# Phi in the place of its transposed softmax, its exponentials in the split keys' place, and the softmax step ahead of the last mixing step

## The chip, the core and the metric

One core of a Trainium2 chip runs the whole kernel as one program. The metric is the device time of one execution in microseconds (us), median of several runs. The engines are TensorE (PE; its weight loads are PEld), VectorE (DVE), ScalarE (ACT), GpSimd (POOL) and SyncE (SP), whose queue issues the DMAs. Each engine works through its own row of instructions in order; between engines they wait for each other.

## What is computed

```python
# q, k, v: (8 batches, 8 heads, 576, 64); phi: (8, 8, 576, 32)
a = exp(phi - max(phi, axis=2)); a = a / (sum(a, axis=2) + 1e-09)      # softmax over the 576 rows
k_m = einsum('bhsm,bhsd->bhmd', a, k); v_m = einsum('bhsm,bhsd->bhmd', a, v)
scores = matmul(q, k_m^T) / sqrt(64); attn = softmax(scores) ; x = matmul(attn, v_m)
X = fft over the 576 rows, then over the 512 columns; u = x + real(X)
un = (u - mean) / sqrt(var + 1e-06)                                    # per row
out = u + relu(un @ w_ch1) @ w_ch2                                     # 512 -> 2048 -> 512
```

Phi's softmax makes 32 memory slots a head; each row of q attends to those 32 slots. The result, all heads side by side, is 8 x 576 rows of 512, mixed by two Fourier transforms, normalized and sent through a two-layer FFN.

## The kernel before

**Tiles and chunks.** The 4608 rows are 36 tiles of 128 rows. A batch gives 4.5 tiles: two mixing steps (`t0`, `t1`) each give two tiles, one for either sign of the frequency, and step `t2` gives half a tile, whose other half comes from the next batch. An even batch mixes `t0`, `t1`, `t2`; an odd batch `t2`, `t0`, `t1`, so that its `t2` completes the tile the even batch began. Two tiles are a chunk, and there are 18 chunks. Chunk 6 is tiles 12 and 13, and tile 13 is completed by batch 3's `t2`; chunk 15 is completed by batch 7's `t2` in the same manner.

**The FFN.** For each chunk `norm_chunk` (L864) normalizes both tiles: ACT makes mean and variance (L853, L854), DVE and POOL the factor (L855 to L859), DVE the normalized tile `un` (L860). Then ACT casts to 16 bits (`ud`, L879), POOL makes the low half (L880), and a DMA transposes both (L882 by L301) into `unring`. The first layer's matmuls `ph` (L318, eight groups of 24 a chunk) read `unring`; ACT and DVE make the high and low half of the relu in `hring` (L939, L940); the second layer's matmuls are `po` (L949). Up to seven hidden blocks of the first layer run ahead of the second.

**Attention and mixing of a batch** are the generator `background()` (L1175), of which the main loop takes a step now and then between the FFN's blocks (`advance`). A batch's steps are in order: the softmax of phi (`pooling_weights`), four pairs of heads (`pair_memory`, then the scores `psc`), `values`, `spectrum` (matmuls `pa`), and three mixing steps (matmuls `pp` for the Fourier part, `px` for the attention part; ACT L818 and DVE L821, L835 add them into the tile).

**The softmax step** `pooling_weights` (L385): four loads bring phi to `phs`; PE transposes (`pf_b_0`, `pf_b_1` with four transposes of 128 columns each, `pl_b` with the rest of both); DVE takes maxima (L398, L403 to L405); ACT makes four exponentials into `pht`, a view of `phs` (L409, L410); DVE sums and inverts (L411 to L415). Then, for g = 0 and 1, ACT and DVE make the high and low half in `elt` (L418, L419), and a DMA transposes `elt` into `et`. There is one `elt`, so its second filling waits for the first transpose. Batches 0 and 1 take another way, in 32 bits.

**Pairs.** `pair_memory` (L516) squares keys, values and queries on ACT to find their size (L526, L529). The squares themselves are dumped into `stg[:, 2]`, where the split keys are to lie later; a matmul with ones (`pm` <- small) adds the sums across partitions, ACT and POOL or DVE split keys and values in halves (L541 to L547), and 20 matmuls `pm` <- `et`, `stg` make the memory.

**Places.** `phs` is reused inside a batch: `stacks[2]` and `stacks[3]`, the transposed scores of pairs 2 and 3, are views of it, and the mixing matmuls `px` read them until the batch's last mixing step. So the loads of the next batch's phi wait for that step. `et` is last read by the `pm` matmuls of a batch's fourth pair.

A framework sorts the instructions into each engine's row beforehand, from the order in which the program issues them and its own estimate of when each can start. So the rows follow the program's order only roughly, and code that is issued elsewhere changes rows of other stages too.

Of the kernel before, what the change touches and what calls it, by code (L numbers as in the profile page):

```python
# [10 lines left out]
F32 = mybir.dt.float32  # L11
# [10 lines left out]
B, H, S, D, M = 8, 8, 576, 64, 32  # L22
NG = H // 2
# [114 lines left out]
def kernel(  # L138
# [70 lines left out]
    def of_kind(t, w):  # L209
        return t[:, :, 1:3] if w else t[:, :, 0::3]  # L210

    qs = [stg[:, 2, 2 * nk + i * NQ : 2 * nk + (i + 1) * NQ] for i in range(2)]
    et32 = et.rearrange("p g l t c -> p (g l t c)").bitcast(F32).rearrange("p (g t c) -> p g t c", g=2, t=NST)


# [107 lines left out]


    def load_phi(b):
        for g in range(NG):
            nc.sync.dma_start(out=phs[:, :, g], in_=raw[b, g, :, KV:KVP].rearrange("p (t c) -> p t c", t=NST))

    def load_pair(b, g):
        r = rawt  # L330
# [53 lines left out]

    def pooling_weights(b):  # L385

        if b:
            load_phi(b)
        pl = psg.tile([P, 512], F32, tag="g", name=f"pl_{b}")
        mx = tiny("mx", 4, 2)  # L390
        pf = []
        for g in range(2):
            pf.append(psg.tile([P, 512], F32, tag="g", name=f"pf_{b}_{g}"))
            for t in range(NST):
                dst = pf[g][:, t * P : (t + 1) * P] if t < 4 else pl[:, g * P : (g + 1) * P]
                marks["pe"] = nc.tensor.transpose(dst, phs[:, t, 2 * g : 2 * g + 2].rearrange("p g c -> p (g c)"), identf)
            if b >= NX:
                nc.vector.tensor_reduce(out=mx[:, g : g + 1], in_=pf[g], axis=AX.X, op=ALU.max)  # L398
        rest = pl[:, : 2 * P].rearrange("p (g s) -> p g s", g=2)[:, :, : S - 4 * P]
# [775 lines left out]
    def background():  # L1175
# [3 lines left out]
        for b in range(B):  # L1179
            n = f"{b}"  # L1180
            ivs = tiny("ivs", NG)
            mem, ahl = {}, {}
            if b != 1:
                pooling_weights(b)
            yield (nt if half_made is None else half_made), 0
            if b == 0:

                for g in range(NG + 1):
# [7 lines left out]
            for step in range(NG + 2) if b > 0 else ():  # L1196
# [7 lines left out]
                if step < NG:  # L1204
                    mem[step] = pair_memory(b, step, r, vmf, ivs)
                    yield (nt if half_made is None else half_made), 0
            vbd, vh, isg, igx, isq = values(b, vmf, ivs, ahl)
            yield (nt if half_made is None else half_made), 0
            at = spectrum(b, aeo)
            if b == 0:  # L1210
# [2 lines left out]
            for g in sorted(ahl):  # L1213
                pair_transpose(b, g, ahl.pop(g), attnT)
            full = slice(0, P)
            for t in (0, 1, 2) if b % 2 == 0 else (2, 0, 1):
                yield (nt if half_made is None else half_made), 2 if t < 2 else 1 - b % 2
                if t == 2:
                    if b % 2 == 0:
                        u2 = uring[:, len(allocs) % NU]  # L1220
                        us[nt] = u2
                        allocs.append(nt)
                        half_made = nt
                        nt += 1
                    rows = slice(64 * (b % 2), 64 * (b % 2) + 64)
                    tm = mix_m(b, "t2", slice(256, 320), rows, at, vh, isg, isq)
                    px = mix_x(b, "t2", 4 * P + 64, 64, rows, attnT, vbd)
                    add_mix(u2, rows, px, igx, tm, 0)
                    half_made = nt - 1 if b % 2 == 0 else None
                    continue  # L1230
                tm = mix_m(b, f"t{t}", slice(t * P, (t + 1) * P), full, at, vh, isg, isg)
                for sign in range(2):
                    c0 = (2 * t + sign) * P
                    px = mix_x(b, f"t{t}{sign}", c0, P, full, attnT, vbd)
                    u = uring[:, len(allocs) % NU]
                    allocs.append(nt)
                    add_mix(u, full, px, igx, tm, sign)
                    us[nt] = u
                    nt += 1
            yield (nt if half_made is None else half_made), 0  # L1240
        while True:
            yield n_tiles, 0
# [209 lines left out]
```

## Time and profile before

| | |
|---|---|
| time, median of 3 runs | 923.89 us (922.73 to 924.33) |
| profiled execution, its own time | 923.03 us |
| its span, first to last instruction | 921.2 us |
| PE busy | 909.5 us, 99% |
| DVE, ACT, POOL busy | 618.0, 492.2, 268.3 us |
| PE's waits for `et` | 2.4 us in three places |
| mean granted clock of TensorE | 0.998 of full speed |

The span is what the trace covers; 1.8 us of the execution lie outside it. PE is nearly always busy. Its busy time counts matmuls from start to modelled end, so that a PE at half its clock also counts as busy: what a stretch was worth is seen in the granted clock beside it (1.00 is the 2.4 GHz level, 0.50 the 1.2 GHz one).

### The profile page before, as it was taken

The numbers are of one execution on the slowest core, as the hardware profiler recorded it, in microseconds if no ns is written. First come the engines' busy times: TensorE is split into PE (matmuls) and PEld (weight loads), VectorE is DVE, ScalarE is ACT, GpSimd is POOL, SyncE is SP. The second block draws the span as 40 slices with busy tenths as digits, with TensorE's granted clock in tenths as the row PEclk, the third lists the DMA queues.
The fourth block names the chain that finished last, engine by engine and source line by source line (L and its number), as shares of the span: only waits on it lengthen the run. The fifth ranks groups of instructions, "written<-read, shape, count | busy, mean of one in ns | idle before, by whom it ended". The sixth has DMA issues, their size and how long they took to land.

```text
span 921.2 us, 19338 instructions
## 1 busy us (share of the span) xinstructions
PE 909.5 (99%) x7796; PEld 671.5 (73%) x7796; DVE 618.0 (67%) x1471; ACT 492.2 (53%) x955; POOL 268.3 (29%) x302
## 2 busy tenths in 40 slices
PE   9999899999999999999999999999999999999998
PEld 8977577677766766776767666777776777688887
DVE  5979967677577775787554767567765776564554
ACT  5658867655464654664444545466546644443331
POOL 1305524124154231463143423144213141400000
PEclk9999999999999999999999999999999999999999
DMA  9938732433336342545123524163416335210000
GB/s 326 413 146 284 208 91 52 97 84 105 60 75 166 76 124 55 144 84 148 40 69 64 159 72 123 41 141 110 96 38 158 76 106 150 47 46 2 24 14 34
DMA packets 132761, 100.16 MB, mean 109 GB/s; under 512 B 115008, under 2 KB 115264, under 8 KB 130624
## 3 DMA queue, kind: packets, MB, share of 16 engines
q1 hardware_dynamic: 132672, 98.93, 39.4%
q8 instruction: 61, 1.00, 0.5%
q14 instruction: 28, 0.23, 0.1%
HBM read 62.35 MB, written 13.63 MB: 82 GB/s over the span
## 4 chain that ended last, share of the span: by engine, by line
PE 79%; DVE 8%; ACT 4%; DMA 3%; issue 3%; POOL 2%; SPq 1%; POOLq 0%; ACTq 0%; DVEq 0%
PE ph L318 32%; PE po L949 26%; PE po L1011 6%; PE pm L318 2%; PE pp_t L318 2%; PE psc L318 2%; PE po L910 1%; PE pa L748 1%; DMA et<-elt 1%; PE ph L893 1%; POOL ud L880 1%; DMA w1t<-in_raw 1%; PE pm L497 1%; PE px_t L318 1%; DVE w2s L1100 1%
## 5 line engine op out<-in xcount | busy, mean ns | idle before, releaser
L318 PE MATMUL ph<-unring,w1t 128*128 128x256 f16 x3264 | 389.7, 273 | 0.0
L318 PEld LDWEIGHTS <-w1t 128*128 128x128 f16 x3264 | 314.9, 98 | 58.0 <-issue 3.1
L949 PE MATMUL po<-w2s,hring 128*128 128x512 f16 x1344 | 309.2, 379 | 0.5 <-DVE uring L1056 0.5
L949 PEld LDWEIGHTS <-hring 128*128 128x128 f16 x1344 | 129.9, 98 | 134.1 <-issue 0.6
L940 DVE SCALAR_TENSOR_TENSOR hring<-ph,hring 128x512 f16<-128x512 f32 x112 | 76.0, 681 | 25.2 <-ACT hring L939 23.7
L939 ACT ACTIVATE hring<-ph 128x512 f16<-128x512 f32 x112 | 65.7, 588 | 47.3 <-PE ph L318 46.9
L859 POOL TENSOR_TENSOR scratch<-scratch,small 128x1 f32<-128x1 f32 x36 | 23.9, 667 | 174.7 <-DVE scratch L858 162.5
L634 POOL TENSOR_TENSOR aring<-aring,scratch 128x384 f32<-128x384 f32 x28 | 26.2, 934 | 164.7 <-DVE scratch L632 141.0
L880 POOL TENSOR_TENSOR ud<-un,ud 128x1024 f16<-128x1024 f32 x17 | 37.2, 2186 | 35.8 <-ACT ud L879 35.8
L318 PEld LDWEIGHTS <-stg 128*128 128x128 f16 x912 | 35.2, 97 | 6.5 <-issue 3.3
L628 ACT ACTIVATE aring<-aring,scratch 128x384 f32<-128x384 f32 x24 | 14.6, 610 | 47.2 <-DVE aring L627 47.1
L658 ACT CAST aeo<-eo 128x384 f16<-128x384 f32 x30 | 15.3, 511 | 42.1 <-DVE eo L655 42.1
L835 DVE SCALAR_TENSOR_TENSOR uring<-px_t,scratch,share 128x256 f32<-128x256 f32 (+1 forms) x80 | 34.2, 477 | 1.5 <-PE px_t L318 1.5
L821 DVE SCALAR_TENSOR_TENSOR share<-pp_t,scratch,small 128x257 f32<-128x257 f32 (+1 forms) x48 | 21.1, 480 | 20.3 <-ACT small L818 20.1
L618 DVE TENSOR_REDUCE scratch<-psc 128x12 f32<-128x384 f32 x32 | 17.6, 552 | 24.6 <-PE pm L318 19.7
L544 POOL TENSOR_TENSOR stg<-rawt,stg 128x640 f16<-128x640 f32 x12 | 18.6, 1548 | 52.9 <-ACT rawt L543 52.8
L910 PE MATMUL po<-w2s,hring 128*128 128x512 f32 x64 | 31.2, 609 | 1.9 <-ACT hring L896 1.9
L646 ACT CAST at<-aring 128x640 f16<-128x640 f32 x28 | 20.2, 722 | 23.4 <-POOL aring L634 23.4
L1033 POOL TENSOR_TENSOR uring<-uring,share 128x256 f32<-128x256 f32 x3 | 2.2, 726 | 102.3 <-ACT share L1030 102.3
L660 DVE SCALAR_TENSOR_TENSOR aeo<-aeo,small,eo 128x128 f16<-128x128 f16 x30 | 24.4, 812 | 10.1 <-ACT aeo L658 10.1
L651 DVE TENSOR_TENSOR eo<-aring 128x128 f32<-128x128 f32 x29 | 25.6, 882 | 7.7 <-POOL aring L649 7.7
L659 POOL TENSOR_TENSOR aeo<-eo,aeo 128x256 f16<-128x256 f32 x30 | 22.4, 748 | 28.0 <-ACT aeo L658 24.8
(320 smaller groups left out, 1560.3 us busy)
## 6 DMA issues: line engine op xcount, KB each, us to landing
out<-uring SPq DMA_DIRECT2D x35, 256.0 KB, 2.3
rawt<-in_raw SPq DMA_DIRECT2D x13, 640.0 KB, 5.0
stg<-in_raw SPq DMA_DIRECT2D x13, 640.0 KB, 4.9
stg<-in_w SPq DMA_DIRECT2D x7, 1024.0 KB, 6.1
rawt<-in_raw SPq DMA_DIRECT2D x15, 384.0 KB, 3.1
stg<-in_raw SPq DMA_DIRECT2D x15, 384.0 KB, 3.2
phs<-in_raw SPq DMA_DIRECT2D x28, 160.0 KB, 3.2
w2s<-in_w SPq DMA_DIRECT2D x4, 1024.0 KB, 10.8
```

The lines of the kernel that those rows point to most:

```text
L318: m = nc.tensor.matmul(out, lhsT=lhsT, rhs=rhs, start=start, stop=stop)
L634: eng.tensor_tensor(out=a, in0=a, in1=sm.unsqueeze(2).to_broadcast([P, 12, M]), op=ALU.mult)
L651: nc.vector.tensor_tensor(out=eo[:, 1:3, 0], in0=ap[:, 1:3, 0], in1=ap[:, 1:3, 1], op=ALU.add)
L660: marks[f"s{b}_{g}"] = nc.vector.scalar_tensor_tensor(out=lo[:, :4], in0=hi[:, :4], scalar=mk[:, 64:65], in1=eov[:, :4], op0=ALU.mult, op1 ...
L835: nc.vector.scalar_tensor_tensor(out=u[rows, hs], in0=px[rows, hs], scalar=igx[rows], in1=tm[rows, w * NJ + half : w * NJ + half + 256], o ...
L859: nc.gpsimd.tensor_tensor(out=rs, in0=rs, in1=half, op=ALU.pow)
L880: marks[f"ul{c}"] = nc.gpsimd.tensor_tensor(out=ud[:, 1], in0=un, in1=ud[:, 0], op=ALU.subtract)
L910: nc.tensor.matmul(po[t], lhsT=h[:, f, t], rhs=w[:, f], start=(j == 0 and f == 0), stop=(j == NW - 1 and f == UB - 1),)
L939: marks["fa"] = nc.scalar.activation(h[:, 0], phv, AF.Relu)
L940: marks["fd"] = nc.vector.scalar_tensor_tensor(out=h[:, 1], in0=phv, scalar=0.0, in1=h[:, 0], op0=ALU.max, op1=ALU.subtract)
L949: nc.tensor.matmul(po[t], lhsT=hs[j][:, lh, f * 2 + t], rhs=w2s[:, j * UB + f, lw, :], start=(j == 0 and f == 0 and i == 0), stop=(j == NW ...
L1011: m = nc.tensor.matmul(po[n], lhsT=h[:, la, a], rhs=b[lb], start=(j == 0 and i == 0 and n in ("p1", "p6", "p5", "p4")), stop=(j == NW - 1 ...
```

## The change

For batches after the first, phi is loaded into `phi_own`, a 32-bit view of `et`, in place of `phs`, and its exponentials are written into `pht_own`, a 32-bit view of the first part of `stg[:, 2]`, in place of the view of `phs`. The loads of batch b+1 are issued in the step of `values(b)`, when `et` has been read. `pooling_weights(b + 1)` is issued in a step of its own ahead of batch b's last mixing step for b from 2 to 6, and for batch 2 at the end of batch 1. The number of steps of a batch stays the same, and so do number and form of the instructions. All lines behind the first hunk get numbers two or three higher.

```diff
+    pht_own = stg[:, 2].bitcast(F32)[:, : 2 * S].rearrange("p (g s) -> p g s", g=2)
     qs = [stg[:, 2, 2 * nk + i * NQ : 2 * nk + (i + 1) * NQ] for i in range(2)]
+    phi_own = et.rearrange("p g l t c -> p (g l t c)").bitcast(F32).rearrange("p (t g c) -> p t g c", t=NST, g=NG)
...
     def load_phi(b):
+        dst = phi_own if b else phs
         for g in range(NG):
-            nc.sync.dma_start(out=phs[:, :, g], in_=raw[b, g, :, KV:KVP].rearrange("p (t c) -> p t c", t=NST))
+            nc.sync.dma_start(out=dst[:, :, g], in_=raw[b, g, :, KV:KVP].rearrange("p (t c) -> p t c", t=NST))
...
     def pooling_weights(b):
 
-        if b:
-            load_phi(b)
+        phi, pht = (phi_own, pht_own) if b else (phs, None)
...
-                marks["pe"] = nc.tensor.transpose(dst, phs[:, t, 2 * g : 2 * g + 2].rearrange("p g c -> p (g c)"), identf)
+                marks["pe"] = nc.tensor.transpose(dst, phi[:, t, 2 * g : 2 * g + 2].rearrange("p g c -> p (g c)"), identf)
...
-            if b != 1:
+            if b == 0:
                 pooling_weights(b)
-            yield (nt if half_made is None else half_made), 0
+            if b < NX:
+                yield (nt if half_made is None else half_made), 0
...
             vbd, vh, isg, igx, isq = values(b, vmf, ivs, ahl)
+            if 0 < b < B - 1:
+                load_phi(b + 1)
...
-            for t in (0, 1, 2) if b % 2 == 0 else (2, 0, 1):
+            for i, t in enumerate((0, 1, 2) if b % 2 == 0 else (2, 0, 1)):
+                if i == 2 and 1 < b < B - 1:
+                    yield (nt if half_made is None else half_made), 0
+                    pooling_weights(b + 1)
                 yield (nt if half_made is None else half_made), 2 if t < 2 else 1 - b % 2
...
+            if b == 1:
+                yield (nt if half_made is None else half_made), 0
+                pooling_weights(2)
             yield (nt if half_made is None else half_made), 0
```

How the rows move is seen in three places. The first is PE's row from batch 3's mixing (`px_3_t..`) and the softmax transposes of batch 4 (`pf_4`, `pl_4`) to chunk 6's first layer (`ph_6_0`). Before, the transposes stand among chunk 5's second layer (`po_5_0`, `po_5_1`), right ahead of `ph_6_0`:

```order
L949 MATMUL po_5_1_4019<-w2s_102,hring_106 128x512
L396 MATMUL pf_4_1_4247<-identf_88,phs_72 128x128 x4
L396 MATMUL pl_4_4239<-identf_88,phs_72 128x128
L318 LDWEIGHTS small_86
L318 MATMUL pm_4_0_4315<-scratch_112,small_86 128x3
L949 LDWEIGHTS hring_106
L949 MATMUL po_5_1_4019<-w2s_102,hring_106 128x512
L949 LDWEIGHTS hring_106
L949 MATMUL po_5_1_4019<-w2s_102,hring_106 128x512
L318 LDWEIGHTS w1t_101
L318 MATMUL ph_6_0_4203<-unring_105,w1t_101 128x256
```

In the changed kernel they stand inside the mixing, and the mixing runs straight into `ph_6_0`:

```order
L320 MATMUL px_3_t01_4090<-vbdt_78,phs_72 128x64
L398 MATMUL pf_4_0_4141<-identf_88,et_74 128x128 x4
L398 MATMUL pl_4_4140<-identf_88,et_74 128x128 x2
L398 MATMUL pf_4_1_4148<-identf_88,et_74 128x128 x4
L320 LDWEIGHTS at_80
L320 MATMUL pp_3_t1_4232<-vh_79,at_80 128x257
...
L320 LDWEIGHTS phs_72
L320 MATMUL px_3_t11_4259<-vbdt_78,phs_72 128x64
L320 LDWEIGHTS w1t_101
L320 MATMUL ph_6_0_4200<-unring_105,w1t_101 128x256
```

The `po_5` matmuls have moved in front of batch 3's mixing; from `px_3_t2` to `ph_6_0` there is none left.

The second is ACT's row at the same place. `un_84` and `ud_85` are the normalized tile and its halves, `small_86` the mixing's scratch. Before, the cast into `ud` (L879) follows the two passes over the tile directly:

```order
L818 ACTIVATE small_86<-pp_3_t2_3931,scratch_112 64x255
L818 ACTIVATE small_86<-pp_3_t0_4059,scratch_112 128x255
L853 ACTIVATE un_84,scratch_112<-uring_87 128x512
L854 ACTIVATE un_84,scratch_112<-uring_87,scratch_112 128x512
L879 CAST ud_85<-un_84 128x1024
L818 ACTIVATE small_86<-pp_3_t1_4136,scratch_112 128x255
L853 ACTIVATE un_84,scratch_112<-uring_87 128x512 x2
L854 ACTIVATE un_84,scratch_112<-uring_87,scratch_112 128x512 x2
L879 CAST ud_85<-un_84 128x1024
L409 ACTIVATE phs_72,scratch_112<-pf_4_0_4240,scratch_112 128x512
```

In the changed kernel the exponentials and the next mixing step's pass stand in between:

```order
L820 ACTIVATE small_86<-pp_3_t2_3935,scratch_112 64x255
L820 ACTIVATE small_86<-pp_3_t0_4063,scratch_112 128x255
L855 ACTIVATE un_84,scratch_112<-uring_87 128x512
L856 ACTIVATE un_84,scratch_112<-uring_87,scratch_112 128x512
L411 ACTIVATE stg_100,scratch_112<-pf_4_0_4141,scratch_112 128x512
L412 ACTIVATE stg_100,scratch_112<-pl_4_4140,scratch_112 128x64
L411 ACTIVATE stg_100,scratch_112<-pf_4_1_4148,scratch_112 128x512
L412 ACTIVATE stg_100,scratch_112<-pl_4_4140,scratch_112 128x64
L820 ACTIVATE small_86<-pp_3_t1_4232,scratch_112 128x255
L881 CAST ud_85<-un_84 128x1024
L420 ACTIVATE elt_73<-stg_100,scratch_112 128x576
```

The cast (now L881) has moved behind the four exponentials (L411, L412) and `pp_3_t1`'s pass.

The third is ACT's row behind batch 3's exponentials. `stg_100` holds split keys and queries, `rawt_71` the loaded ones. Before, the split of pair 0 (L541, L603) stands ahead of the first `elt`, its squares still further ahead:

```order
L409 ACTIVATE phs_72,scratch_112<-pf_3_1_3013,scratch_112 128x512
L410 ACTIVATE phs_72,scratch_112<-pl_3_3005,scratch_112 128x64
L541 ACTIVATE stg_100<-rawt_71,scratch_112 128x5x2x64
L541 ACTIVATE stg_100<-rawt_71,scratch_112 128x5x128
L603 ACTIVATE stg_100<-rawt_71,scratch_112 128x768
L418 ACTIVATE elt_73<-phs_72,scratch_112 128x576
L939 ACTIVATE hring_106<-ph_4_0_2969 128x512
L543 ACTIVATE rawt_71<-rawt_71,scratch_112 128x5x128
L939 ACTIVATE hring_106<-ph_4_1_3048 128x512
L969 CAST ud_85<-un_84 128x1024
L418 ACTIVATE elt_73<-phs_72,scratch_112 128x576
```

In the changed kernel the squares of pair 0 (L528, L531) come only behind the second `elt`, and the split (L543) behind those:

```order
L420 ACTIVATE elt_73<-stg_100,scratch_112 128x576
L941 ACTIVATE hring_106<-ph_4_0_2977 128x512
L941 ACTIVATE hring_106<-ph_4_1_3048 128x512
L420 ACTIVATE elt_73<-stg_100,scratch_112 128x576
L528 ACTIVATE stg_100,scratch_112<-rawt_71 128x5x2x64
L528 ACTIVATE stg_100,scratch_112<-rawt_71 128x5x128
L531 ACTIVATE stg_100,scratch_112<-rawt_71 128x768
L971 CAST ud_85<-un_84 128x1024
L941 ACTIVATE hring_106<-ph_4_2_3132 128x512
L941 ACTIVATE hring_106<-ph_4_3_3213 128x512
L543 ACTIVATE stg_100<-rawt_71,scratch_112 128x5x2x64
```

What stood beside the softmax's chain has moved behind it.

## Rows read from the trace of the kernel before

**Rows 1.** The page: span, and busy time of PE (share, instructions).

```profile
span 921.2 us, 19338 instructions
...
PE 909.5 (99%) x7796; PEld 671.5 (73%) x7796; DVE 618.0 (67%) x1471; ACT 492.2 (53%) x955; POOL 268.3 (29%) x302
```

**Rows 2.** Waits of PE: releaser: us in total, times, longest.

```profile
PE pm L318 <- DMA et<-elt: 2.4, 3, 1.9
```

**Rows 3.** Timeline of PE, batch 3: start, duration, instruction, [idle before <- releaser].

```profile
280.80 0.69 PE L318 MATMUL pm<-et,stg 128*128 128x64 f16 x20 [1.91 <-DMA et<-elt]
```

**Rows 4.** Windows: from:to, length, busy PE, PEld, DVE, ACT, POOL, PEclk, DMA share, GB/s.

```profile
281.80:282.80 1.00, 1.00 (x8) 0.76 (x6) 0.96 (x3) 1.00 (x4) 0.00 (x0) 0.60 0.91 293
282.80:283.80 1.00, 1.00 (x7) 0.72 (x5) 0.51 (x3) 1.00 (x5) 0.00 (x0) 0.50 1.00 371
283.80:284.80 1.00, 1.00 (x7) 0.69 (x6) 0.58 (x2) 0.61 (x2) 0.00 (x0) 0.50 1.23 344
284.80:286.00 1.20, 1.20 (x10) 0.96 (x9) 1.20 (x2) 0.00 (x0) 0.00 (x0) 0.74 1.14 220
```

**Rows 5.** Timeline of PE: last softmax transpose of batch 3.

```profile
266.20 0.27 PE L396 MATMUL pl<-identf,phs 128*128 128x128 f32 x1
```

**Rows 6.** Tile `et`: who waited for it, us in total, times.

```profile
  ACT elt L418: 18.9, 6
```

**Rows 7.** Timeline of PE, batch 3 mixing to chunk 6.

```profile
352.80 0.29 PE L318 MATMUL px_t<-vbdt,phs 96*64 96x64 f16 x4
353.02 1.49 PE L318 MATMUL pp_t<-vh,at 128*128 128x257 f16 x12
354.34 0.28 PE L318 MATMUL px_t<-vbdt,attnT 96*128 96x64 f16 x4
...
354.58 3.40 PE L949 MATMUL po<-w2s,hring 128*128 128x512 f16 x15
...
366.96 0.60 PE L396 MATMUL pf<-identf,phs 128*128 128x128 f32 x4
...
367.51 0.81 PE L949 MATMUL po<-w2s,hring 128*128 128x512 f16 x3
...
369.16 1.03 PE L318 MATMUL ph<-unring,w1t 128*128 128x256 f16 x8
```

**Rows 8.** Timelines of DVE, ACT and POOL in the same stretch, in this order.

```profile
357.75 0.55 DVE L860 TENSOR_SCALAR un<-uring,scratch 128x512 f32<-128x512 f32 x1 [0.66 <-POOL scratch L859]
358.26 0.88 DVE L835 SCALAR_TENSOR_TENSOR uring<-px_t,scratch,share 128x256 f32<-128x256 f32 x2
...
358.33 1.04 ACT L879 CAST ud<-un 128x1024 f16<-128x1024 f32 x1 [1.64 <-DVE un L860]
359.57 0.47 ACT L818 ACTIVATE small<-pp_t,scratch 128x255 f32<-128x255 f32 x1 [0.19 <-PE pp_t L318]
...
359.46 2.13 POOL L880 TENSOR_TENSOR ud<-un,ud 128x1024 f16<-128x1024 f32 x1 [1.74 <-ACT ud L879]
```

**Rows 9.** Tile `unring`: its transposes from issue to landing.

```profile
DMA to landing us min/median/max: 3.6/4.2/5.6
```

**Rows 10.** Timelines: a maximum (DVE), exponentials of two pairs (ACT, batch 2).

```profile
367.60 0.69 DVE L398 TENSOR_REDUCE scratch<-pf 128x1 f32<-128x512 f32 x1 [1.38 <-PE pf L396]
...
167.15 0.69 ACT L409 ACTIVATE phs<-pf,scratch 128x512 f32<-128x512 f32 x1 [1.97 <-DVE scratch L405]
...
168.12 0.68 ACT L409 ACTIVATE phs<-pf,scratch 128x512 f32<-128x512 f32 x1
```

**Rows 11.** Timelines of POOL and DVE in batch 2; line L404: min/median/max ns.

```profile
164.77 2.12 POOL L1161 TENSOR_TENSOR w2s<-w2s 128x1024 f16<-128x1024 f32 x1 [1.30 <-ACT w2s L1160]
...
164.89 2.02 DVE L404 TENSOR_TENSOR scratch<-scratch 128x2 f32<-128x2 f32 x1
...
L404 DVE TENSOR_TENSOR scratch<-scratch x6: 153/161/2025, 164.9 to 699.8; 128x2 f32<-128x2 f32 x6
```

**Rows 12.** Timeline of PE: second layer ahead of chunk 15.

```profile
786.16 10.74 PE L949 MATMUL po<-w2s,hring 128*128 128x512 f16 x49
```

## The prediction

> **What bounds the kernel now.** I read the busy times first: PE works 909.5 of 921.2 us [rows 1], so a change gains only what PE idles or runs slowly, and loses whatever makes PE idle anew. Second, the waits of PE: the one that this change is aimed at, `pm` waiting for the transposed softmax `et`, is 2.4 us in three places, 1.9 of it in batch 3 [rows 2]. Third, the windows, which show a price that the waits hide: behind that 1.9 us idle [rows 3] the granted clock, full in the 25 us ahead, falls to 0.60, 0.50, 0.50 and 0.74 in four neighbouring windows [rows 4]. That is 0.80 + 1.00 + 1.00 + 0.62 = 3.4 us at the lower level (1.2 instead of 2.4 GHz), in which half is lost: 1.7 us. All that can be won at `et` is therefore 2.4 + 1.7 = **4.1 us**. Last, I read where PE is next to idle: at the first matmul of a chunk's FFN, which needs that chunk's normalized tiles. Nothing waits there in this run, because other PE work lies between; how much does is what the change alters.
>
> **What the change takes away.** Phi of the next batch no longer waits for the last mixing step to leave `phs`. In batch 3 the last softmax transpose ends at 266.20 + 0.27 = 266.5 and the `et` matmuls start at 280.8: the chain takes 14.3 us [rows 3, 5], and PE has 12.4 of work in it. In the changed order the PE work between the same two points, counted in matmuls at the widths and pitches of these rows, is 21 us or more in batches 2, 3, 5, 6 and 7, so the wait goes there: -2.4 - 1.7 = **-4.1 us**. In batch 4 it is only about 11.5, which by itself would leave 3, but that stretch holds the new wait computed below, which covers it. The instructions themselves are the same in number and form; of the four loads a batch, SP has none that stands in front of a transpose PE needs soon: 0.
>
> **What it adds: a wait for the split keys' place.** The squares of pair 0 (`pair_memory`) write into `stg[:, 2]`, which now holds the exponentials until the second `elt` is made, and this waits for the first `et` transpose (ACT already waits 18.9 us there in six steps [rows 6]). So the conversion of pair 0 no longer runs beside the softmax: the ones-matmul of pair 0 in batch 3 moves from right behind the softmax transposes to 16 us of PE work later, and the whole attention of batch 3 ends some 15 us later in PE's row. The four later steps from ones-matmul to `et` matmuls keep 4.4 us of PE work or more, as pairs 1 to 3 have today without a wait: no cost of its own. But what is late next is the mixing of batch 3, and with it chunk 6, whose second tile is finished by `px_3_t2`.
>
> **Chunk 6, the term that decides.** Today 53 `po` matmuls of chunk 5 lie between `px_3_t2` and `ph_6_0`, and PE is occupied from 353.09 to 369.16, 16.1 us [rows 7]. In the new order chunk 5 is used up before `pp_3_t2`, and between the two stand only two mixing products, four sets of `px`, and the ten transposes of the softmax step, which is now in front of the last mixing step. By starts in the rows: 353.02 to 354.34 = 1.32 a product; 354.34 to 354.58 = 0.24 a set; 366.96 to 367.51 = 0.55 for five transposes [rows 7]. 2 x 1.32 + 4 x 0.24 + 2 x 0.55 = **4.7 us** of work.
> Against it stands the chain from `px_3_t2` to the landing of `unring`. Today: DVE normalizes until 358.30, ACT casts until 359.37, POOL makes the low half until 361.59 [rows 8], that is 361.59 - 353.09 = 8.5 us; with the transpose's 4.2 us [rows 9] 12.7. In the new order two things stand inside it. On DVE two maxima over 512 columns (0.69 each), one over the rest, two small operations (0.16 each) and two additions that came later before (0.88) stand ahead of the normalization; with 0.3 for the smaller maximum (an estimate: a quarter of the columns and the start) that is 2 x 0.69 + 0.3 + 0.32 + 0.88 = 2.9, of which 0.4 fills a gap, so 2.5 [rows 8, 10, 11]. On ACT the exponentials of two pairs (one pair 167.15 to 168.12, so 1.94 [rows 10]) and one `L818` (0.47 [rows 8]) stand ahead of the cast; the exponentials wait for the last maximum, and the normalization runs beside the first half of them, so 1.5 remains. Chain: 12.7 + 2.5 + 1.5 = 16.7; PE is out of work after 4.7: **+12.0 us**. Lower end: if nothing of the softmax step delays it, 12.7 - 4.7 = 8.0. Upper end: +1.4 if the transpose lands in 5.6 instead of 4.2 [rows 9], and +1.9 as follows.
> One row shows that a DVE operation over two columns, of 0.16 us normally, took 2.02 us, from 164.89 to 166.91, while POOL ran from 164.77 to 166.89 [rows 11]: it ended when POOL did. The same operation is now in the normalization's way; 2.02 - 0.16 = 1.9. I take 0, since POOL's row at that place has only the step that waits for this normalization. The Trainium skill, SBUF — State Buffer, section SBUF: two separate sides, says that a DVE operation with two SBUF inputs and a GpSimd operation that reads SBUF take a shared port pair in turn, and the loser stands still for the whole instruction; the row agrees, and by this rule the sum would become 1.9 larger if POOL were busy there.
> An idle of 12 us at `ph_6_0` is longer than the 1.9 of batch 3, and I give it the same price in clock: **+1.7 us** (no less; 0 only if the clock stays).
> The first `relu` of chunk 6 then stands on ACT behind the second `elt` and the squares. These need no PE work, so they run on while PE is idle for the 12 us, and that idle is their cover: 0, or 2 us if the cover is a little short (an estimate: three squares, each about an exponential's 0.69 [rows 10]).
>
> **Chunk 15** is finished by `px_7_t2` in the same way. Between it and `ph_15_0` stand two products, four sets and 36 `po` matmuls; 49 of these take 10.74, 0.22 each [rows 12]: 2.64 + 0.96 + 7.9 = 11.5 us. Its chain has none of the softmax in it, so 12.7: **+1.2 us**; bounds 0 and 1.2 + 1.4 (slow landing) + 1.7 (clock). The smallest such distance of another chunk is about 15, against 12.7: no wait.
>
> **Sum.** -4.1 + 12.0 + 1.7 + 1.2 = +10.8 us. The profiled execution took 923.03 (span 921.2), so 933.8; the median 923.89 lies 0.86 above it: **934.7 us**.
>
> **Rivals.**
> A (the sum), 934.7: 0.62.
> B, the other side: the `et` waits go and chunk 6's chain is covered, 923.9 - 4.1 = 919.8. It is one place, `ph_6_0`, and turns on the exposure there staying under about 4 us, that is on a chain below 8.8 us. For it: PE is as good as never idle in this profile. Against it: cast, low half and transposition alone are 1.0 + 2.1 + 4.2 = 7.3 of it, and nothing in the new order could give PE more than 4.7 us of work: 0.07.
> C, only the unavoidable part: 8.0 at chunk 6 with the clock, none at 15: -4.1 + 9.7 = +5.6, 929.5; without the clock 927.8. For it: DVE and ACT have gaps in these rows into which the softmax step may fall: 0.18.
> D, all upper ends: 1.9 + 1.4 at chunk 6 and 1.4 + 1.7 at chunk 15: +10.8 + 6.4 = +17.2, 941.1. For it: one landing in the list took 5.6; against: they must coincide: 0.10.
> E, the change doesn't do what it says: the `et` chain finds its load or its exponentials late again in batch 3, and the 4.1 us stay: 938.9. For it: `elt` is still single, and its second half still waits for a landing; against: 21 us of work against 14.3: 0.03.
>
> **How the numbers follow.** Likeliest A: 934.7. The range from 927 to 941 takes in C with and without the clock, E, and nearly all of D; B and the far end of D are left out. About 0.2% (1.85 us) is what a measurement here can tell from no change. Faster is most of B, 0.06; within 0.2% the rest of B and the lower edge of C, 0.04; slower A, most of C, D and E, 0.90.
>
> **What would show it.** Right: no `pm <- et` wait in batches 2 and 3; a wait of PE at the first `ph` of chunk 6 of 10 to 14 us with the `unring` transpose named last; 16 to 17 us from `px_3_t2` to it, with the maxima and exponentials inside; a half-clock stretch of 3 to 4 us behind it; a small wait at chunk 15. Wrong: FFN matmuls of chunk 5 still running between `px_3_t2` and `ph_6_0`, or an idle below 5 us there, which is B; an idle of 8 with the cast right behind the normalization is C; a new wait at another engine that I have not named would make the sum itself wrong.

## The result and the profile after

The changed kernel takes 936.52 us (median of 4 runs, 936.16 to 936.62), the one before 923.31 beside it (4 runs): ratio 1.0142, interval 1.0125 to 1.016. It is slower by 13.2 us. The forecast was 934.7, range 927 to 941. The profiled execution took 936.61 us with a span of 934.8, 13.6 more than the span before.

The first view to read is again the list of PE's waits, now of the changed kernel (engine, line, what it waited for: us in total, times, longest us):

```profile
PE ph L320 <- DMA unring<-ud: 11.8, 1, 11.8
...
PE ph L320 <- DVE un L862: 1.5, 1, 1.5
PE pa L742 <- DVE aeo L662: 1.3, 1, 1.3
PE pm L320 <- ACT stg L543: 0.8, 1, 0.8
```

The waits for `et` [rows 2] are gone. In their place stands one wait of 11.8 us at the first layer, and behind it small ones: 1.5 at the first layer again (this is chunk 15), 1.3 at `pa` in batch 1 and 0.8 at `pm` in batch 3, the last two new and not forecast. The rows left out are short or stand in the kernel before with nearly the same length. The long one in PE's timeline (start us, duration, instruction, idle before and what ended it), with the rows that answer to [rows 7]:

```profile
364.92 0.29 PE L320 MATMUL px_t<-vbdt,phs 96*64 96x64 f16 x4
...
369.73 0.28 PE L320 MATMUL px_t<-vbdt,phs 96*128 96x64 f16 x4
381.77 8.06 PE L320 MATMUL ph<-unring,w1t 128*128 128x256 f16 x48 [11.76 <-DMA unring<-ud]
```

`px_3_t2` ends at 364.92 + 0.29 = 365.21. PE has work until 370.01, which is 4.8 us, and chunk 6 starts at 381.77: the chain took 16.56 us. Where the kernel before has 53 `po` matmuls in between there is none left.

What the chain is made of, in the timelines of DVE, ACT, POOL and SP in this order (they answer to [rows 8]):

```profile
371.93 0.55 DVE L862 TENSOR_SCALAR un<-uring,scratch 128x512 f32<-128x512 f32 x1 [0.32 <-POOL scratch L861]
...
371.70 0.69 ACT L411 ACTIVATE stg<-pf,scratch 128x512 f32<-128x512 f32 x1 [2.88 <-DVE scratch L407]
...
373.97 1.06 ACT L881 CAST ud<-un 128x1024 f16<-128x1024 f32 x1
...
375.11 2.13 POOL L882 TENSOR_TENSOR ud<-un,ud 128x1024 f16<-128x1024 f32 x1 [3.22 <-ACT ud L881]
...
377.27 1.78 SPq L303 DMA_TRANSPOSE unring<-ud  x1
```

The tile is normalized at 371.93 + 0.55 = 372.48, 7.3 us behind `px_3_t2` (5.2 before). The first exponential starts at 371.70, and the cast, ready at 372.48, waits for the exponentials until 373.97. POOL's low half ends at 377.24, the transpose is issued at 377.27 and PE starts 4.5 us later.

Behind the wait stands the slow stretch, in the windows (from:to, length, busy time of PE, PEld, DVE, ACT and POOL, then the granted clock, DMA share, GB/s):

```profile
372.00:374.00 2.00, 0.00 (x0) 0.00 (x0) 0.67 (x3) 2.00 (x10) 0.00 (x0) 0.90 0.00 0
...
382.00:384.00 2.00, 2.00 (x11) 1.40 (x10) 0.02 (x1) 1.74 (x2) 0.96 (x1) 0.50 0.32 59
384.00:386.00 2.00, 2.00 (x12) 1.34 (x11) 1.78 (x1) 0.18 (x1) 1.92 (x2) 0.50 0.00 0
386.00:388.00 2.00, 2.00 (x14) 1.53 (x13) 0.00 (x0) 2.00 (x5) 1.92 (x2) 0.69 0.49 95
```

From 381.77 the clock is at the lower level for 0.23 + 2.00 + 2.00 + 1.24 = 5.5 us, 2.7 lost. It had fallen while PE stood idle: 0.90 from 372 to 374, 0.50 from there on. In [rows 4] the stretch was 3.4 us, behind a shorter idle, and it began only when PE had worked again for 1 us (from 280.80 to 281.80 the clock is 1.00).

The sum against the profile before: -2.4 and -1.7 at `et`, +11.8 at chunk 6, +2.7 of clock, +1.5 at chunk 15, +1.3 at `pa`, +0.8 at `pm`; the other small waits come to about -0.6. Together 13.4 of the 13.6 us.

### The profile page after: what moved, and what is told of

It is laid out like the page before. It is cut to its first block, busy times and chain, and to the rows that moved or that the text cites. A ratio compares the mean times of both kernels' runs of the same rounds, so it can differ in the third digit from the quotient of the medians.

```text
span 934.8 us, 19333 instructions
## 1 busy us (share of the span) xinstructions
PE 910.9 (97%) x7796; PEld 670.8 (72%) x7796; DVE 619.1 (66%) x1471; ACT 494.5 (53%) x955; POOL 267.6 (29%) x302
## 4 chain that ended last, share of the span: by engine, by line
PE 88%; DVE 4%; ACT 3%; DMA 2%; issue 1%; SPq 1%; POOL 1%; ACTq 0%
PE ph L320 37%; PE po L951 30%; PE po L1013 6%; PE pm L320 2%; PE pp_t L320 2%; PE psc L320 2%; PE po L912 1%; PE pa L750 1%; PE ph L895 1%; DMA w1t<-in_raw 1%; PE px_t L320 1%; PE pm L499 1%; DMA et<-elt 1%; PE pp_t L801 1%; DVE w2s L1102 1%
## 5 line engine op out<-in xcount | busy, mean ns | idle before, releaser
L320 PE MATMUL ph<-unring,w1t 128*128 128x256 f16 x3264 | 390.4, 274 | 13.2 <-DMA unring<-ud 11.8
L823 DVE SCALAR_TENSOR_TENSOR share<-pp_t,scratch,small 128x257 f32<-128x257 f32 (+1 forms) x48 | 21.1, 480 | 24.3 <-ACT small L820 24.2
L837 DVE SCALAR_TENSOR_TENSOR uring<-px_t,scratch,share 128x256 f32<-128x256 f32 (+1 forms) x80 | 34.2, 476 | 1.2 <-PE px_t L320 1.1
L546 POOL TENSOR_TENSOR stg<-stg 128x640 f16<-128x640 f32 x12 | 19.3, 1607 | 50.6 <-ACT stg L545 50.6
L895 PE MATMUL ph<-unring,w1t 128*128 128x256 f32 x128 | 30.6, 383 | 0.0
```

The source lines that it names most:

```text
L320: m = nc.tensor.matmul(out, lhsT=lhsT, rhs=rhs, start=start, stop=stop)
L546: nc.gpsimd.tensor_tensor(out=lo, in0=kinds[w], in1=hi, op=ALU.subtract)
L837: nc.vector.scalar_tensor_tensor(out=u[rows, hs], in0=px[rows, hs], scalar=igx[rows], in1=tm[rows, w * NJ + half : w * NJ + half + 256], o ...
L895: nc.tensor.matmul(ph, lhsT=w[:, k, f * P : (f + 1) * P], rhs=unTs[0][:, k], start=(k == 0), stop=(k == NK - 1))
```

## The experiments

**Theory.** Pair 0's squares and split wait for the place in which the exponentials lie. This moves a batch's attention back in PE's row by some 15 us, and the FFN work that covered the next chunk's normalization is used up before it is needed. **Rival.** The softmax step, now ahead of the last mixing step, stands inside the normalization's chain and lengthens it. Besides, what phi's own place is worth was to be seen alone. The change has three parts, which the runs put together in different ways:

| kernel | phi in | exponentials in | softmax step | us |
|---|---|---|---|---|
| before | `phs` | `phs` | behind the last mixing step | 923.3 to 923.5 |
| run e5 | `phs` | split keys' place | behind | 968.05 |
| run e1 | `et` | split keys' place | behind | 960.92 |
| changed | `et` | split keys' place | ahead | 936.52 |
| run e6 | `et` | `phs` | behind | 919.47 |
| run e2 | `et` | scores' ring | ahead | 919.48 |
| run e3 | `et` | scores' ring | ahead of the first mixing step | 925.28 |

**Both places, the order as before.**

```diff
-                if i == 2 and 1 < b < B - 1:
-                    yield (nt if half_made is None else half_made), 0
-                    pooling_weights(b + 1)
...
-            if b == 1:
+            if 0 < b < B - 1:
                 yield (nt if half_made is None else half_made), 0
-                pooling_weights(2)
+                pooling_weights(b + 1)
```

> The changed kernel, but the softmax step of the next batch stands behind the batch's last mixing step, as before; phi in et and the exponentials in the split keys' place stay. Theory (the new wait for the split keys' place starves PE): slower still than the changed kernel. In PE's row only 4.5, 4.8 and 5.6 us of work stand between the finishing mix and the first layer of chunks 6, 13 and 15, and 11.7 at chunk 11, against a chain of 12.7 without the softmax in it: idles of about 8.2, 7.9, 7.1 and 1.0, each of the first three with 2 to 3 us of lost clock, so 923.3 - 4.1 + 24 + 8 = about 951 us. Rival (the softmax step inside the normalization's chain is what costs): the chain is free of it again, so 920 to 924 us.

Measured: 960.92 us, ratio to the kernel before 1.0405 (1.0389 to 1.0422). PE's waits:

```profile
PE ph L320 <- DVE un L862: 11.4, 1, 11.4
PE ph L320 <- DMA unring<-ud: 11.4, 2, 9.6
PE ph L320 <- ACT un L856: 11.1, 1, 11.1
```

Three waits of 9.6 to 11.4 us at the first layer (chunks 6, 13 and 15), and a fourth of 1.9 (chunk 11), where the changed kernel has one long and one of 1.5. So the softmax step's new order isn't what costs; without it the kernel is 24 us slower still. The theory's direction held, its size didn't: it allowed 7 to 8 us a wait, because it took the chain for 12.7 us when the softmax isn't in it. Chunk 15 shows that this is too little: no softmax step follows batch 7, and yet its chain takes 15.4 us, from the end of `px_7_t2` at 820.58 to

```profile
827.79 0.54 DVE L862 TENSOR_SCALAR un<-uring,scratch 128x512 f32<-128x512 f32 x1
...
835.99 2.31 PE L320 MATMUL ph<-unring,w1t 128*128 128x256 f16 x10 [9.57 <-DMA unring<-ud]
```

The tile is normalized 7.8 us behind `px_7_t2`, where it takes 5.2 at chunk 15 of the changed kernel. Run e4 shows what stands in between.

**The exponentials in a place of their own.**

```diff
-    pht_own = stg[:, 2].bitcast(F32)[:, : 2 * S].rearrange("p (g s) -> p g s", g=2)
+    pht_own = aring.rearrange("p n c m -> p (n c m)")[:, : 2 * S].rearrange("p (g s) -> p g s", g=2)
```

> The changed kernel, but the exponentials lie in the scores' ring aring, which is idle there, instead of in the split keys' place; the order in which the steps are issued stays. Theory: pair 0 no longer waits, chunk 6 gets 13.6 us of PE work in front of it against 16.7 with the softmax in its chain (idle up to 3), and the et matmuls of batches 4 and 6 have 12.7 and 12.6 us against 14.3 (idle up to 1.7 each): 923.3 - 4.1 + 3 + 3.4 = about 925, between 919 and 929. Rival (the softmax step's place costs it): chunk 6 idles 8 us or more as in the changed kernel, 930 to 937 us.

Measured: 919.48 us, ratio 0.9955 (0.994 to 0.9971), better than expected and faster than both kernels. The order in which the steps are issued is that of the changed kernel; only the place differs. Behind the first 140 us PE's waits are these alone:

```profile
PE psc L320 <- DVE scratch L589: 0.8, 2, 0.4
```

Neither the wait at chunk 6 nor one for `et` is left, so the order of issue alone doesn't cost. It doesn't settle by itself what the softmax step costs inside the chain, because here it isn't inside. DVE's row at chunk 6:

```profile
354.20 0.55 DVE L862 TENSOR_SCALAR un<-uring,scratch 128x512 f32<-128x512 f32 x1 [0.67 <-POOL scratch L861]
...
355.50 0.68 DVE L400 TENSOR_REDUCE scratch<-pf 128x1 f32<-128x512 f32 x1
```

The normalization stands ahead of the maxima and ends at 354.75, 5.2 us behind `px_3_t2` (349.54) as in the kernel before; with FFN matmuls between the mixing steps the framework orders the row the other way round. That price is for run e4.

**The same, the softmax step ahead of the first mixing step** (`if i == 0` in place of `if i == 2`).

> As the run with the exponentials in the scores' ring, and the softmax step is issued ahead of the batch's first mixing step instead of its last. Theory: 16.8 us of PE work in front of chunk 6, 15.3 to 17.7 at chunks 4, 11, 13 and 15, 19 us or more ahead of the et matmuls of batches 3 to 7 (15.0 in batch 2): neither wait is left, 923.3 - 4.1 = about 919 us, 918 to 922. Rival (softmax in front of mixing lengthens the chain): 927 us or more.

Measured: 925.28 us, ratio 1.0026 (1.0015 to 1.0038). The expectation missed by 6 us: `et` and chunk 6 are free as expected, but other waits came up.

```profile
PE psc L320 <- DVE scratch L589: 3.5, 3, 1.6
```

There is also one of 1.4 us at `po`. What those at `psc` hang on is seen in batch 3, POOL's and DVE's timelines:

```profile
274.91 2.12 POOL L962 TENSOR_TENSOR un<-w2s 128x1024 f32<-128x1024 f16 x1
...
274.95 2.37 DVE L579 TENSOR_SCALAR vmf<-scratch 64x32 f32<-64x32 f32 x2
277.24 0.74 DVE L589 TENSOR_TENSOR scratch<-scratch 128x64 f16<-128x64 f32 x1
```

Two small DVE operations take 2.37 us together, until 277.32, while a POOL operation runs from 274.91 to 277.03; the scores' `psc` wait for the operation that follows. The two other waits at `psc` have the same rows: the DVE pair takes 2.38 us from 375.86 beside POOL's 375.83 to 377.95, and 2.37 from 605.41 beside 605.38 to 607.50. So it is where POOL's long operations fall, moved by the new order, and not the chain of chunk 6. The wait at `po` wasn't followed.

**Batch 3 alone with the softmax step behind.**

```diff
-                if i == 2 and 1 < b < B - 1:
+                if i == 2 and 1 < b < B - 1 and b != 3:
...
-            if b == 1:
+            if b in (1, 3):
                 yield (nt if half_made is None else half_made), 0
-                pooling_weights(2)
+                pooling_weights(b + 1)
```

> The changed kernel, but in batch 3 alone the softmax step of batch 4 stands behind the last mixing step. PE's work in front of chunk 6 is 4.5 us as in the changed kernel. Theory: only the part of the chain that the softmax step adds goes, 16.6 to about 12.7, so the idle at chunk 6 falls from 11.8 to about 8.2 and the time from 936.5 to about 933 us. Rival: the whole idle goes, about 923 us.

Measured: 935.46 us, ratio 1.0128 (1.011 to 1.0146), one us less than the changed kernel. PE's, DVE's and ACT's timelines:

```profile
364.94 0.29 PE L320 MATMUL px_t<-vbdt,phs 96*64 96x64 f16 x4
...
381.11 8.08 PE L320 MATMUL ph<-unring,w1t 128*128 128x256 f16 x48 [11.08 <-DVE un L862]
...
370.33 0.47 DVE L823 SCALAR_TENSOR_TENSOR share<-pp_t,scratch,small 128x257 f32<-128x257 f32 x1
...
371.11 0.68 DVE L400 TENSOR_REDUCE scratch<-pf 128x1 f32<-128x512 f32 x1
371.71 1.26 DVE L837 SCALAR_TENSOR_TENSOR uring<-px_t,scratch,share 128x256 f32<-128x256 f32 x3
372.88 0.54 DVE L862 TENSOR_SCALAR un<-uring,scratch 128x512 f32<-128x512 f32 x1
...
373.45 1.04 ACT L881 CAST ud<-un 128x1024 f16<-128x1024 f32 x1 [4.27 <-DVE un L862]
```

The chain from `px_3_t2` (365.23) is 15.88 us, 0.7 less than in the changed kernel, not 4. The cast now follows the normalization at once, 373.45 behind 373.42. But the normalization itself ends 8.2 us behind `px_3_t2` instead of 7.3: the additions of the last mixing step (L823, L837), which PE reaches sooner, and one maximum now stand ahead of it in DVE's row. PE's row has no FFN work left there, so the mixing results come one after the other, and the framework has put DVE's work on them in front. Together with chunk 15 of run e1 this says that the lack of work lengthens the chain by itself. (The profile names DVE's `un` as what ended PE's wait; that belongs to the next chunk, whose first tile was normalized at the same moment. The transpose of this chunk was issued at 376.72, and the shortest in this stretch landed in 4.2 us, at about 380.9.)

**The exponentials' place alone**, as an edit of the kernel before.

```diff
+    pht_own = stg[:, 2].bitcast(F32)[:, : 2 * S].rearrange("p (g s) -> p g s", g=2)
...
     def pooling_weights(b):
 
+        pht = pht_own if b else None
         if b:
             load_phi(b)
```

> The kernel before with one edit: the exponentials of batches 2 to 7 are written into the split keys' place; phi stays in phs, its loads and the softmax step stay where they were. Theory (this place alone makes the loss): PE's work in front of the first layer is 8.2, 4.5, 4.1 and 5.8 us at chunks 4, 6, 13 and 15 and 12.5 at chunk 11, against a chain that took some 16 us where such a lack of work was measured: idles of about 8, 11, 11, 10 and 3, clock on top, the et waits gone, so about 971 us, 955 to 980. Rival (phi's place or the order makes it): within 3 us of 923.

Measured: 968.05 us, ratio 1.0486 (1.0462 to 1.0509).

```profile
PE ph L319 <- DMA unring<-ud: 20.1, 5, 9.0
PE pf L398 <- DMA phs<-in_raw: 7.2, 3, 3.8
```

This one edit, without the others, costs 45 us. Part of the idle is booked at `pf`, which stands next in PE's row and waits for phi's late loads; the expectation had put all of it at the first layer, and its sum held within 3 us.

**Phi's place alone**, as an edit of the kernel before: `load_phi` writes to `phi_own` and is issued in the step of `values`, the transposes read it there; exponentials and order stay.

```diff
+        dst = phi_own if b else phs
...
-        if b:
-            load_phi(b)
+        phi = phi_own if b else phs
...
+            if 0 < b < B - 1:
+                load_phi(b + 1)
```

> The kernel before with one edit: phi of the next batch is loaded into et in the step of values; exponentials back in phs, the softmax step behind the last mixing step as before. Theory: no lack of work (14.9, 16.4, 17.7, 17.2, 16.6 us in front of chunks 4, 6, 11, 13, 15), but the softmax starts no earlier, so the et matmuls have 11.6 to 15.0 us of work against a chain of 14.3: waits of 0 to 2.7 us as before, 921 to 928 us, about 924. Rival (late loads are what the et waits are made of): the waits go, about 919 us.

Measured: 919.47 us, ratio 0.996 (0.9948 to 0.9973). The rival was right here: this part alone wins 4 us. The softmax transposes of batch 3 and the `et` matmuls:

```profile
259.40 0.60 PE L397 MATMUL pf<-identf,et 128*128 128x128 f32 x4
...
274.97 0.69 PE L319 MATMUL pm<-et,stg 128*128 128x64 f16 x20 [1.38 <-DMA et<-elt]
```

From 260.0 to 275.0 the chain takes 15.0 us, and the wait of 1.38 is the only one left for `et`; no half-clock stretch follows it (the mean granted clock of the run is 1.000). Batch 5, for which the expectation counted 11.6 us of work, does not wait at all: its `et` matmuls start 11.4 us behind the last softmax transpose (492.17 to 503.53), so its chain is shorter than the 14.3 us that [rows 3, 5] gave for batch 3. The expectation had priced every batch by the slowest.

**PE kept busy at chunk 6.**

```diff
+FILL = 105
...
+        if b == 3 and key == "t2":
+            marks["px"] = marks["pe"]
...
+        if c == 6 and j == 0:
+            with tc.issue_after(marks["px"].ins):
+                for _ in range(FILL):
+                    nc.tensor.matmul(ph[:, 0], lhsT=unread[:, :P], rhs=unread, start=True, stop=True)
```

> The changed kernel with 105 matmuls more, of no use, into the first layer's bank of chunk 6 behind the px of batch 3's t2: PE is busy while it waits for the chunk's normalized tiles. Theory (behind the idle PE runs at the lower clock, and this costs 2.8 us): the chain stays at some 16 us, the half-clock stretch goes, and 0.8 us of mixing that now stands behind the wait comes on top: about 934.5 us. Rival (the clock's drop costs nothing at the end): 936.5 to 937.5 us.

Measured: 936.55 us (ratio 1.0145, 1.0125 to 1.0166), the changed kernel's time. The windows show that the clock did stay up:

```profile
382.00:384.00 2.00, 2.00 (x33) 1.84 (x31) 1.52 (x1) 0.42 (x1) 1.92 (x2) 1.00 0.00 0
384.00:386.00 2.00, 2.00 (x25) 1.79 (x22) 0.00 (x0) 1.99 (x6) 1.96 (x1) 1.00 0.38 75
```

and waits that take back a part of the gain:

```profile
PE pm L321 <- ACT stg L544: 1.4, 3, 0.8
...
PE psc L321 <- ACT scratch L589: 0.9, 2, 0.6
PE pm L321 <- ACT stg L532: 0.4, 1, 0.4
```

The wait at chunk 6 is gone and the clock full. At `pm` and `psc` PE now waits 1.4 + 0.9 + 0.4 us, against 0.8 in the changed kernel: 1.9 us more, in batches 4 and 6. That looks like the rival, but the edit has a flaw: part of the 105 matmuls stand between the softmax transposes of batch 4, whose last ends at 371.79 and not at 368.23 as in the changed kernel, and batch 3's last mixing step falls behind the filling too (its last `px` ends at 384.16, not 370.01). This alone can make batch 4 late. The next run avoids it.

**PE kept busy behind the mixing.**

```diff
                     add_mix(u, full, px, igx, tm, sign)
+                    if b == 3 and t == 1 and sign == 1:
+                        fill = ps2.tile([P, 512], F32, tag="o", name="fill")
+                        with tc.issue_after(marks["pe"].ins):
+                            for _ in range(80):
+                                nc.tensor.matmul(fill[:, : 2 * P], lhsT=unread[:, :P], rhs=unread, start=True, stop=True)
```

> The changed kernel with 80 matmuls more, of no use, behind the last px of batch 3 and ahead of chunk 6's first layer: 80 x 0.109 = 8.7 us of the 11.8 us wait are filled, about 3 us of idle are left, and unlike in the first filled run the softmax transposes of batch 4 stay where they were. Theory (the clock's drop costs 2.7 us at the end, and the first filled run hid that by delaying the softmax transposes): if the clock stays up, 934 us; if it still falls behind the 3 us of idle, 935 to 936. Rival (the attention of batch 4 is late next and takes back what the clock gives): clock up, and 936 to 937 us with waits of 1.5 us or more at pm and psc of batch 4.

Measured: 935.88 us (ratio 1.013, 1.0108 to 1.0151), 0.6 less than the changed kernel.

```profile
365.23 0.29 PE L320 MATMUL px_t<-vbdt,phs 96*64 96x64 f16 x4
...
370.16 8.90 PE L1250 MATMUL fill<-identf 128*128 128x256 f16 x80
382.08 7.07 PE L320 MATMUL ph<-unring,w1t 128*128 128x256 f16 x48 [3.02 <-DMA unring<-ud]
...
382.00:384.00 2.00, 1.92 (x14) 1.61 (x15) 0.20 (x1) 1.59 (x2) 0.65 (x1) 0.78 0.47 90
384.00:386.00 2.00, 2.00 (x12) 1.39 (x11) 1.74 (x1) 0.22 (x1) 1.92 (x2) 0.50 0.00 0
386.00:388.00 2.00, 2.00 (x18) 1.71 (x17) 0.09 (x1) 1.88 (x5) 2.00 (x1) 0.87 0.32 63
```

From `px_3_t2` (365.52) to the first layer it takes 16.56 us, exactly as in the changed kernel. Behind the 3.0 us of idle that are left the clock is at the lower level for 0.88 + 2.00 + 0.52 = 3.4 us instead of 5.5, which saves 1.0 us, and the profiled execution is 0.8 us shorter (935.85 against 936.61), with `px_3_t2` 0.3 later. No wait at `pm` or `psc` of batch 4 takes it back. So what the clock gives reaches the end, as far as 0.8 us can show it (the ratios' intervals overlap), and the waits of the first filled run are most likely its own delay of the softmax transposes.

**A second `elt`**, which frees the split keys' place one landing sooner: the second half goes to a view of the scores' ring.

```diff
-            nc.scalar.activation(elt[:, 0, :S], pht[:, g], AF.Copy, scale=r)
+            el = elts[g]
+            if g:
+                nc.gpsimd.memset(el[:, :, S:], 0.0)
+            nc.scalar.activation(el[:, 0, :S], pht[:, g], AF.Copy, scale=r)
...
```

> The changed kernel with a second elt (in the scores' ring) for the second half, so that the split keys' place is free one transpose's landing sooner. Theory (the length of that wait sets the lack of work): PE's work in front of chunk 6 grows from 4.5 to 6.9 us, at chunk 15 from 11.2 to 16.7; the idle at chunk 6 falls from 11.8 to about 9.4 and the one of 1.5 at chunk 15 goes: about 932.5 us. Rival (the wait's length doesn't matter, only that pair 0 stands behind the softmax): 936 us.

Measured: 930.64 us, ratio 1.0079 (1.0057 to 1.01), 5.9 us less than the changed kernel.

```profile
PE ph L321 <- DMA unring<-ud: 8.3, 1, 8.3
```

The wait at chunk 6 shrank by 3.5 us with the place's shorter occupation, the one at chunk 15 is gone. PE has 7.2 us of work in front of it where the changed kernel has 4.8. Shorter wait for the place, less lack of work: the theory again, with more gain than it allowed.

## Why the prediction was right, and where its steps were off

**The et waits**, -2.4 and -1.7: right. They are gone in the changed kernel, and the runs e2 and e6, which have nothing of the loss, gain 4.0 us. That this is so near the 4.1 of the sum is in part luck: e6 keeps 1.4 us of the wait, and a wait of 0.5 at `po` in the kernel before is gone in both. What brings the gain is phi's place, not the order: e6 has the order of before.

**The new wait for the split keys' place**: right as the cause. The exponentials' place alone costs 45 us (e5), taking it away returns all (e2), shortening it returns part (e8). In the changed kernel's batch 3 the wait stands in ACT's row, and pair 0's ones-matmul behind it in PE's:

```profile
281.54 0.74 ACT L528 ACTIVATE stg<-rawt 128x640 bf16<-128x640 f32 x1 [1.37 <-DVE elt L421]
...
284.63 0.17 PE L320 MATMUL pm<-scratch,small 128*128 128x3 bf16 x1
```

The first square starts when DVE has made the second `elt`. The ones-matmul follows 16.6 us behind the last softmax transpose (267.99); before, it stood right behind it (266.31), and the prediction said 16. What the runs don't separate is the wait itself from the framework's foresight of it: no run has the exponentials in this place with pair 0's rows kept where they were.

**Chunk 6**, +12.0: 11.8 measured, with 4.8 us of work (4.7 in the sum) against a chain of 16.56 (16.7). The total is right: DVE adds 2.1 us (2.5 in the sum), the cast waits 1.5 (1.5), and the transpose takes 0.3 more, so two small errors cancel. One step behind it is only half right. The sum charged 4.0 us of the chain to the softmax step and took 12.7 us as what is left without it; that was the lower end of 8.0 and rival C. In e4, without the exponentials ahead of the cast, 15.9 us are left, and 15.4 at chunk 15 of e1, which has no softmax near it. With FFN matmuls between the mixing steps the chain is 12.7 in the kernel before and 12.9 at chunk 15 of the changed kernel. Once PE has none, the additions of the next mixing step stand in DVE's row ahead of the normalization. So moving the softmax alone could not have given C.

**The clock**, +1.7: a term of the right kind, mis-sized. The half-clock stretch behind the idle was 5.5 us and not the 3.4 of [rows 4], which is 2.7 us. The prediction took the price behind 1.9 us of idle for one of 12. Nor is 5.5 a fixed price: behind idles of 8.3 to 11.8 us the stretch lasted between 3.0 (e8) and 5.9 us (chunk 13 of e1), not in the order of the idles. That the term reaches the end is what e9 speaks for, where a shorter stretch came off the profiled time; its size at the end wasn't measured by itself.

**Chunk 15**, +1.2: 1.5 measured, with 11.45 us of work (11.5 in the sum) against a chain of 12.9 (12.7).

**Not in the sum**: +1.3 at `pa` in batch 1 and +0.8 at `pm` in batch 3. By the prediction's own last sign, a new wait that it had not named, the sum was wrong here. These two and the clock's 1.0 more than explain why the forecast fell 1.8 us short. The first is the contention that the prediction priced for chunk 6 and took at 0 there. POOL's, DVE's and PE's timelines of the changed kernel in batch 1:

```profile
120.00 2.13 POOL L1126 TENSOR_TENSOR w1t<-w1t 128x1024 f16<-128x1024 f32 x1 [0.26 <-ACT w1t L1125]
...
120.36 1.92 DVE L662 SCALAR_TENSOR_TENSOR aeo<-aeo,small,eo 128x128 f16<-128x128 f16 x1 [1.46 <-ACT aeo L660]
...
122.33 0.30 PE L742 MATMUL pa<-ct,aeo 128*128 128x290 f16 x1 [1.27 <-DVE aeo L662]
```

and the same DVE and POOL operations of the kernel before:

```profile
120.07 0.57 DVE L660 SCALAR_TENSOR_TENSOR aeo<-aeo,small,eo 128x128 f16<-128x128 f16 x1 [1.40 <-ACT aeo L658]
...
121.17 2.13 POOL L1124 TENSOR_TENSOR w1t<-w1t 128x1024 f16<-128x1024 f32 x1
```

The DVE operation took 1.92 us, until 122.28, beside a POOL operation that ended at 122.13, and PE waited for it; before, it took 0.57 and POOL's long operation began only behind it. What moved POOL forward is the change: the squares of batch 2's first pair stood in ACT's row here (at 114.57 in the kernel before) and are now behind the softmax, so that ACT hands POOL its work a microsecond sooner. That this comes with the exponentials' place fits the other runs: e1, e4, e5, e7, e8 and e9, which have them there, wait 1.2 to 1.3 us at this `pa`, e2 and e3 0.2, e6 not at all.

The second wait, for pair 0's split (L543), has the same kind of rows behind it, in POOL's and DVE's timelines of batch 3:

```profile
287.34 2.12 POOL L962 TENSOR_TENSOR un<-w2s 128x1024 f32<-128x1024 f16 x1 [6.45 <-DVE ud L973]
...
287.90 1.58 DVE L289 TENSOR_SCALAR scratch<-scratch 128x3 f32<-128x3 f32 x1
```

This DVE operation, on the way from the ones-matmul to the split, usually takes 0.16 us (the median of 26); here it took 1.58 and ended at 289.48, POOL's at 289.46. The 1.4 us are more than the 0.8 that PE waited. So the distance that the prediction priced at 0, here 5.7 us of PE work, would have been enough without it.

**Rivals.** B (the chain covered) and E (the `et` waits staying) are excluded by the waits; D's price of a held DVE operation was paid, at two other places. C is not what happened: 11.8 us of idle, not 8, and the cast behind the exponentials.

## What to carry to other kernels

A buffer that is free when its new owner writes it may still be needed soon: look who writes it next, and what that work had run beside. In a kernel whose main engine is at 99%, count the work that stands in its row between a producer and its consumer, against the chain between them; the row of the changed program gives this before anything is run, and here it gave the wait to 0.2 us, with small errors that cancelled. But take the chain as it runs when that work is gone: here 15 to 16 us, and 12.7 with the work beside it. A bundle of edits is best taken apart: one of three parts made all of the gain, another all of the loss, and the third only softened it.

## What was not expected of the hardware

Small DVE operations were held for a whole POOL operation in several of these kernels, 0.16 to 2.02 us [rows 11], 0.57 to 1.92 in batch 1, 0.16 to 1.58 in batch 3, two in 2.37 in run e3; in batch 1 a shift of 1.2 us in POOL's row decided it. The Trainium skill, SBUF — State Buffer, section SBUF: two separate sides, describes a shared port pair that whichever of the two engines starts first holds for its whole instruction: a GpSimd operation, or a DVE operation that runs in a two-port mode or, against a GpSimd operation that reads SBUF, has two SBUF inputs. The first two rows have two inputs and agree, POOL having started first and DVE's ends lying within 0.15 us of POOL's; the operations of batch 3 and of run e3 have one tensor input, and whether they ran in such a mode no trace shows. The clock's half-speed stretch lasted 3.4 us behind idles of 1.9 [rows 3, 4] and 3.0 us (run e9), where the clock was still full when PE resumed and fell about 1 us later; behind the idle of 11.8 us it had fallen during the idle and stayed low for 5.5 us more. The idle of 1.38 us in run e6 left it full.
